# Carried key transposes from unit 6 on, in a gated linear attention and gated MLP kernel with a hand-written early order

## The chip, the cores and the metric

The kernel runs on one core of a Trainium2 chip. The metric is the device time of one execution in microseconds. Five engines each work through a queue of their own: TensorE (PE, its weight loads shown apart as PEld), VectorE (DVE), ScalarE (ACT), GpSimd (POOL) and SyncE (SP), which here only issues DMAs.

## What is computed

```python
def _attn_ref(q, k, v, alpha):            # q, k, v, alpha: [4, 8, 768, 48]
    for t in range(S):
        state = alpha[:, :, t, :, None] * state + np.einsum('bhd,bhe->bhde', k[:, :, t], v[:, :, t])
        y[:, :, t] = np.einsum('bhd,bhde->bhe', q[:, :, t], state)

def _moe_ref(x, w_gate, w_val, w_out):    # x: [3072, 384], d_ff 1536
    gate = 1.0 / (1.0 + np.exp(-(x @ w_gate)))
    return (gate * (x @ w_val)) @ w_out
```

The attention's output, heads side by side, is the MLP's x.

## The kernel before

The 3072 tokens are cut into 6 groups of 512, the 8 heads into 4 pairs. A group and a pair make a **unit**, 24 in all: units 0 to 3 are group 0, units 4 to 7 group 1, units 8 to 11 group 2. In a unit the recurrence is done in chunks: two scans along the tokens on VectorE give the decays G (L422) and F (L426), keys are multiplied by G (L430) and queries by F (L523 in units 0 to 3, L616 later), TensorE makes the scores in a chunk (L535, L632) and the sums of keys and values (L540, L638), VectorE masks the scores (L548, L648), the sums are carried from chunk to chunk (a scan, L450, up to unit 9; eight steps, L670, from unit 10), ScalarE puts the scaled states in place (L563, L659), and TensorE makes the outputs (L575 and L580, or L693).

The MLP is 72 **steps**: 6 groups by 12 tiles of d_ff. A step makes the gate's and the value's product (gv, L245, 18 matmuls of 512 columns), a sigmoid, a product, a split into a high part hh and a low part hl, and 9 matmuls back into po (L738). x has a high and a low part too; for group 0 VectorE makes the low one at L589, one for each of units 1 to 3. Steps 0 and 1 are cut in three by these parts of x.

The weights come as 64-bit numbers, a tile of d_ff in two pieces (tile 0 in three). Each piece is loaded (L374), its top bits are cast (L379 on ScalarE, or L377 on VectorE for pieces listed in CASTS), a word is put together (L382), the high part cast (L385) and the low part subtracted (L393). All of this is done in the first 114 us, along with units 0 to 9, while steps 0 to 11 already run. Raw pieces go round in a ring of four buffers (later three), so a load waits until an older piece's low part is done.

**Keys with tokens on the partitions.** The sums need the decayed keys transposed. Units 0 to 9 do it by `turn` (L460): four 128x128 transposes on TensorE (L464) into a PSUM bank and a copy by ScalarE (L468). Units 10 to 23 do it by `carry` (L472): VectorE transposes 32x32 blocks (L474), one DMA writes them to a way tile in DRAM (L477), and four DMAs bring them back in the right places (L481), in runs of 32 floats.

**Order.** Every piece of work is a numbered part of a plan with an engine, a planned cost, a due time and what it reads and writes. For each engine the table ORDER lists the parts that it runs first, by number, for about the first 140 us; the rest is ordered by planned costs and due times. KEYS and QUERIES name the units whose key or query product runs on VectorE and not on GpSimd. WARM is the number of matmuls on nothing that fill TensorE's queue in the first 30 us.

Numbers in ORDER that matter here (up to 426 the same in both kernels): 119 low x of unit 2, 90 of unit 1, 148 of unit 3 (L589); 329 to 334 the thirds of step 0 and 345 to 350 those of step 1; 316 scores and sums of unit 4; 307 transposes of unit 4. Behind 426 the changed kernel counts four more for each of units 6 to 9.

```python
        if u < 2 * NP:
            t = dict.fromkeys(("load", "more", "G", "dec", "kt", "q", "kn", "X", "A", "mask", "S", "sd", "out", "y"))
            return late(u, g, p, {**t, "flag": 14.0 + u})
...
        if u >= CARRIED:
            t.update(first=x - 0.6, turn=x - 0.4, away=x - 0.2, back=x + 0.6)
...
        carried = "turn" in t
        if carried:
            knn, kn = carry(t, inn, kT, gn, G)
        else:
            pkn, pk = r_gv.next()
            knn, kn = turn(t, inn, kT, pkn, pk)
```

Of the kernel before, what the change touches and what calls it, by code (L numbers as in the profile page):

```python
# [19 lines left out]
B, H, S, D = 4, 8, 768, 48  # L20
# [177 lines left out]
def scan(n):  # L198
    return n / 450
# [6 lines left out]
def act(n):  # L206
    return 0.01 + n / 1065
# [41 lines left out]
def chunked(ctx, tc, rows, vc, vh, vg, weights_in, out, const, ident, flags, weights, within):  # L249
# [185 lines left out]
    def through(u, g, p, t, nch, decn, ends, banks):  # L435
# [6 lines left out]
        plan.add("scalar", 0.09 + act(D * m), t["dec"], lambda: nc.scalar.copy(  # L442
# [4 lines left out]
        for i, (bn, bank) in enumerate(banks):  # L447
            plan.add("scalar", 0.09 + act(D * nch // len(banks)), t["S"], lambda i=i, bank=bank: nc.scalar.copy(
                out=chunks(add, 1 - first + i, m, len(banks)), in_=bank), [bn], [(dn, i)])
        plan.add("vector", 0.09 + scan(D * m), t["S"], lambda: nc.vector.tensor_tensor_scan(  # L450
            out=sd, data0=add, data1=rep, initial=0.0, op0=ALU.add, op1=ALU.mult), [rn, (dn, "i"), *((dn, i) for i in range(2))], [sn], port=True)
        plan.add("gpsimd", 0.25, t["S"], lambda: nc.gpsimd.tensor_tensor(
# [104 lines left out]
    def in_place(u, p, t, qT, inn, vw, A, states):  # L557
# [3 lines left out]
        for j in range(2):  # L561
            r = slice(R * j, R * j + R)
            plan.add("scalar", 0.09 + act((CH - 1) * D), t["sd"], lambda j=j, r=r: nc.scalar.copy(  # L563
                out=sd[r, 1:CH, D * j:D * j + D].rearrange("p c e -> p e c"), in_=some(1, CH)[r].rearrange("p c e -> p e c")), [sn], [(sdn, 2 * j), (sdn, 2 * j + 1)])
# [28 lines left out]
    def late(u, g, p, t):  # L593
# [61 lines left out]
        if u < SCANNED:  # L655
            sn, some = through(u, g, p, t, EH, decn, dec, [
                (pn, bank[:, T // 2:T // 2 + CH * D].rearrange("p (c e) -> p c e", e=D)) for pn, bank in pas])
            for j in range(2):
                plan.add("scalar", 0.09 + act(EH * D), t["sd"], lambda j=j: nc.scalar.copy(  # L659
                    out=vs[own[j], j].rearrange("p c e -> p e c"), in_=some(0, EH)[own[j]].rearrange("p c e -> p e c")), [sn], [(vsn, 2 + j)])  # L660
# [117 lines left out]
    def begin(u):  # L778
# [5 lines left out]
        if u < 2 * NP:  # L784
            t = dict.fromkeys(("load", "more", "G", "dec", "kt", "q", "kn", "X", "A", "mask", "S", "sd", "out", "y"))
            return late(u, g, p, {**t, "flag": 14.0 + u})
# [54 lines left out]
    with tc.manual_schedule():  # L841
# [4 lines left out]
CASTS = ((7, 1), (9, 0))  # L846
QUERIES = (0, 4)
WHOLE = ()
KEYS = (0, 1, 2, 3, 8, 10)
# [10 lines left out]
    ),  # L860
    "vector": (
# [8 lines left out]
    ),  # L870
    "scalar": (
# [6 lines left out]
    ),  # L878
    "gpsimd": (
        5, 2, 3, 72, 0, 56, 101, 4, 1, 130, 305, 312, 374, 141, 367, 322, 326, 83, 388, 112, 432, 392, 425, 486, 493, 449, 453, 554, 510, 514, 623, 779, 611,  # L880
        618, 627, 703, 764, 781,
    ),
    "sync": (
# [7 lines left out]
CARRIED = 10  # L891
# [166 lines left out]
```

## Time and profile before

| | |
|---|---|
| median of 3 runs | 508.27 us (507.75 to 508.96) |
| profiled execution | 508.6 us |
| its span | 506.9 us |
| TensorE busy | 497.2 us (98%) |
| VectorE busy | 322.6 us (64%) |
| ScalarE busy | 193.4 us (38%) |
| GpSimd busy | 85.5 us (17%) |
| TensorE's granted clock, mean over the span | 0.997 |

The profile is of one execution. Its span runs from the first to the last instruction that it shows; 1.7 us lie around it. Shares over the whole span mix two stages: up to about 114 us the weights are unpacked and units 0 to 9 are worked, and behind that only the MLP's steps and the later units are left. A row of a timeline gives start, duration, engine, line, what is written and read, and how many instructions are merged in it. Ends of matmuls are modelled and overlap the next one, so how long TensorE is taken by something is read from start to start.

### The profile page before, as it was taken

The numbers are of one execution on the slowest core, as the hardware profiler recorded it, in microseconds if no ns is written. First come the engines' busy times: TensorE is split into PE (matmuls) and PEld (weight loads), VectorE is DVE, ScalarE is ACT, GpSimd is POOL, SyncE is SP. The second block draws the span as 40 slices with busy tenths as digits, with TensorE's granted clock in tenths as the row PEclk, the third lists the DMA queues.
The fourth block names the chain that finished last, engine by engine and source line by source line (L and its number), as shares of the span: only waits on it lengthen the run. The fifth ranks groups of instructions, "written<-read, shape, count | busy, mean of one in ns | idle before, by whom it ended". The sixth has DMA issues, their size and how long they took to land.

```text
span 506.9 us, 10590 instructions
## 1 busy us (share of the span) xinstructions
PE 497.2 (98%) x4263; PEld 424.7 (84%) x4263; DVE 322.6 (64%) x597; ACT 193.4 (38%) x375; POOL 85.5 (17%) x103
## 2 busy tenths in 40 slices
PE   8999999999999999999999999999999999999995
PEld 3788888888888888888888888888888888888884
DVE  7998989897467956757757658558565432222221
ACT  2888867865323323223233223223322122311221
POOL 3423222211004302203303203112011010000000
PEclk9999999999999999999999999999999999999998
DMA  8797897852553655634535725535733000100001
GB/s 305 264 296 233 274 256 244 249 154 71 127 144 94 152 113 135 154 97 104 132 76 134 196 52 153 123 65 152 166 90 74 12 6 17 63 0 0 1 2 65
DMA packets 81318, 63.92 MB, mean 126 GB/s; under 512 B 62064, under 2 KB 67696, under 8 KB 81264
## 3 DMA queue, kind: packets, MB, share of 16 engines
q1 hardware_dynamic: 81264, 63.20, 45.6%
q8 instruction: 34, 0.56, 0.5%
q14 instruction: 20, 0.16, 0.1%
HBM read 45.62 MB, written 8.39 MB: 107 GB/s over the span
## 4 chain that ended last, share of the span: by engine, by line
PE 88%; ACT 3%; DMA 3%; DVE 3%; issue 1%; SPq 1%; DVEq 0%; ACTq 0%
PE gv L245 51%; PE po L738 26%; PE gv L693 4%; PE at L632 2%; DMA raw<-in_w_dram 2%; PE po L580 1%; PE at L638 1%; DMA x<-yt 1%; ACT vs L659 1%; PE po L575 1%; ACT w L385 1%; DMA in<-in_rows_dram 1%; DVE G L422 0%; PE at L535 0%; DVE sd L450 0%
## 5 line engine op out<-in xcount | busy, mean ns | idle before, releaser
L245 PE MATMUL gv<-x,w 128*128 128x512 f32 x1296 | 300.9, 380 | 0.0
L245 PEld LDWEIGHTS gv<-x,w 128*128 128x128 f32 x1296 | 244.0, 189 | 35.2 <-issue 0.4
L728 DVE TENSOR_TENSOR gv<-gv,sg 128x512 f32<-128x512 f32 x72 | 50.3, 698 | 128.3 <-PE gv L245 121.1
L738 PE MATMUL po<-hh,w 128*128 128x512 f32 x432 | 111.0, 384 | 0.1
L738 PEld LDWEIGHTS po<-hh,w 128*128 128x128 f32 x432 | 79.8, 189 | 12.4 <-ACT hh L729 0.8
L729 ACT CAST hh<-gv 128x512 fp32r<-128x512 f32 x72 | 42.1, 585 | 122.6 <-DVE gv L728 112.2
L726 ACT ACTIVATE sg<-gv 128x512 f32<-128x512 f32 x72 | 43.0, 597 | 113.6 <-PE gv L245 113.5
L677 POOL TENSOR_TENSOR vs<-st,dec 64x384 f32<-64x384 f32 x28 | 29.8, 1063 | 228.6 <-PE gv L245 227.5
L730 DVE TENSOR_TENSOR hl<-gv,hh 128x512 fp32r<-128x512 f32 x72 | 49.1, 681 | 23.1 <-ACT hh L729 19.8
L738 PE MATMUL po<-hl,w 128*128 128x512 f32 x216 | 62.5, 380 | 0.3 <-DVE hl L730 0.3
L738 PEld LDWEIGHTS po<-hl,w 128*128 128x128 f32 x216 | 40.7, 189 | 6.6 <-DVE hl L730 0.9
L648 DVE TENSOR_TENSOR A<-at,mask 64x256 f32<-64x256 f32 x80 | 33.6, 420 | 4.8 <-PE at L638 3.3
L422 DVE TENSOR_TENSOR_SCAN G<-in,d1g 128x512 f32<-128x512 f32 x22 | 31.2, 1418 | 7.6 <-DMA in<-in_rows_dram 7.6
L670 DVE SCALAR_TENSOR_TENSOR st<-st,dec,at 128x48 f32<-128x48 f32 x112 | 29.7, 265 | 3.7
L430 POOL TENSOR_TENSOR in<-in,G 128x512 f32<-128x512 f32 x18 | 24.7, 1370 | 19.7 <-DVE G L422 12.9
L426 DVE TENSOR_TENSOR_SCAN F<-in,d1f 128x512 f32<-128x512 f32 x22 | 27.8, 1264 | 0.2
L693 PE MATMUL gv<-A,vs 112*48 112x64 f32 (+1 forms) x640 | 22.8, 222 | 0.9 <-ACT vs L659 0.8
L693 PEld LDWEIGHTS gv<-A,vs 112*48 112x48 f32 (+1 forms) x640 | 19.4, 123 | 3.9 <-ACT vs L659 2.3
L457 ACT ACTIVATE F<-F 128x512 f32<-128x512 f32 x23 | 14.5, 633 | 4.5 <-DVE in L616 4.4
L632 PEld LDWEIGHTS at<-A,in 48*64 48x64 f32 x640 | 11.2, 134 | 5.9 <-issue 5.6
L616 POOL TENSOR_TENSOR in<-in,F 128x512 f32<-128x512 f32 x6 | 10.0, 1667 | 33.5 <-DVE F L426 33.5
L489 ACT COPY yt<-gv 128x512 f32<-128x512 f32 x20 | 11.7, 587 | 9.5 <-PE gv L693 9.4
(140 smaller groups left out, 339.1 us busy)
## 6 DMA issues: line engine op xcount, KB each, us to landing
in<-in_rows_dram SPq DMA_DIRECT2D x20, 772.5 KB, 5.0
raw<-in_w_dram SPq DMA_DIRECT2D x14, 577.0 KB, 4.9
A<-in SPq DMA_DIRECT2D x40, 128.0 KB, 2.5
first_w<-in_w_dram SPq DMA_DIRECT2D x8, 577.0 KB, 5.0
out_dram<-raw SPq DMA_DIRECT2D x18, 256.0 KB, 2.4
v<-in_vc_dram SPq DMA_DIRECT2D x20, 192.0 KB, 2.7
vs<-in_vh_dram SPq DMA_DIRECT2D x40, 96.0 KB, 3.4
way<-G SPq DMA_DIRECT2D x14, 256.0 KB, 3.2
```

Source lines behind the costliest of these rows:

```text
L245: nc.tensor.matmul(out=dst, lhsT=lhs(a, i), rhs=rhs(b, i), start=(n == 0 and i == 0), stop=(n == len(todo) - 1 and i == NK - 1))
L422: plan.add("vector", scan(n), t["G"], lambda: nc.vector.tensor_tensor_scan(out=G[:, ::-1], data0=az[:, n:0:-1], data1=d1g[size], initial=0 ...
L426: plan.add("vector", scan(n), after(t["G"], 0.01), lambda: nc.vector.tensor_tensor_scan(out=F, data0=az[:, 0:n], data1=d1f, initial=0.0, o ...
L648: plan.add("vector", 0.43, t["mask"], lambda pa=pa, j=j, i=i: nc.vector.tensor_tensor(out=A[other[j], j].rearrange("p (c i t) -> p i c t", ...
L670: nc.vector.scalar_tensor_tensor(out=st[:, c + 1, :], in0=st[:, c, :], scalar=dec[:, c:c + 1], in1=pas[c % 2][1][:, T // 2 + c // 2 * D:T ...
L677: plan.add("gpsimd", pool_(EH * D), t["sd"], lambda j=j: nc.gpsimd.tensor_tensor(out=vs[own[j], j], in0=st[own[j], 0:EH], in1=dec[own[j], ...
L693: nc.tensor.matmul(out=py[R * j:R * j + D, cs], lhsT=vs[r, j, c, :], rhs=A[r, j, cs], start=True, stop=True)
L726: plan.add("scalar", act(T), first(0.3), lambda: nc.scalar.activation(out=sg, in_=got["g"][1][:, 0:T], func=AF.Sigmoid), [got["g"][0]], [sgn])
L728: plan.add("vector", vec(T), first(0.4), lambda: nc.vector.tensor_tensor(out=pv, in0=pv, in1=sg, op=ALU.mult), [sgn], [pvn])
L729: plan.add("scalar", act(T), first(0.45), lambda: nc.scalar.copy(out=hh, in_=pv), [pvn], [hhn])
L730: plan.add("vector", vec(T), first(0.5), lambda: nc.vector.tensor_tensor(out=hl, in0=pv, in1=hh, op=ALU.subtract), [pvn, hhn], [hln])
L738: nc.tensor.matmul(out=pso_now[m][1][:, 0:T], lhsT=weights.part("o", b, f)[:, m * P:(m + 1) * P], rhs=halves(h[a]), start=(f == 0 and i == ...
```

## The change

- CARRIED goes from 10 to 6: units 6 to 9 use `carry` in place of `turn`. Units 6 and 7, which have no due times, get empty ones for its parts.
- KEYS: the key product of unit 4 and of unit 11 goes to VectorE, that of units 3, 8 and 10 to GpSimd. QUERIES: the query product of unit 2 goes to VectorE (the entry 4 has no effect in either kernel, since only units 0 to 3 ask).
- CASTS: the VectorE casts are those of pieces 10.1 and 11.1, not of 7.1 and 9.0.
- Five planned costs are changed; they issue nothing themselves.
- ORDER is new for all five engines. In VectorE's list the third low x (148) stands behind the query product of unit 2 (99 and 101 are unit 2's key and query product), the key product (305) and the 8-column product (304) of unit 4, the reciprocal and the F scan of unit 5 (364, 365) and both word steps of tile 2 (187, 181), which stood behind it or were not VectorE's. In TensorE's list the scores of unit 4 (316) stand ahead of the last thirds of step 0 (331, 334) and step 1 (347, 350). The state scans of units 6 and 7 (L450) stand two weight tiles earlier and one piece-pair earlier in VectorE's list. On SP the return transfers of unit 6 stand behind the loads of pieces 5.0 (215) and 5.1 (221).

```diff
         if u < 2 * NP:
             t = dict.fromkeys(("load", "more", "G", "dec", "kt", "q", "kn", "X", "A", "mask", "S", "sd", "out", "y"))
+            if u >= CARRIED:
+                t.update(dict.fromkeys(("first", "turn", "away", "back")))
             return late(u, g, p, {**t, "flag": 14.0 + u})
...
-CASTS = ((7, 1), (9, 0))
-QUERIES = (0, 4)
+CASTS = ((10, 1), (11, 1))
+QUERIES = (0, 2, 4)
...
-KEYS = (0, 1, 2, 3, 8, 10)
+KEYS = (0, 1, 2, 4, 11)
...
     "tensor": (
...
-        34, 105, 10, 132, 86, 87, 134, 88, 135, 115, 116, 117, 329, 307, 332, 144, 145, 146, 330, 333, 345, 346, 347, 334, 331, 316, 348, 349, 350, 339, 340,
...
+        132, 31, 32, 86, 87, 135, 33, 88, 115, 116, 134, 117, 34, 307, 144, 329, 145, 330, 146, 332, 345, 316, 346, 333, 331, 334, 348, 349, 341, 347, 350,
...
     "vector": (
...
-        153, 107, 154, 157, 111, 300, 166, 137, 90, 301, 140, 159, 302, 160, 303, 169, 136, 119, 171, 362, 172, 363, 175, 148, 187, 177, 304, 364, 178, 365,
...
+        107, 108, 159, 163, 154, 300, 165, 160, 301, 304, 166, 140, 169, 302, 305, 303, 171, 136, 90, 119, 137, 362, 172, 363, 175, 364, 187, 365, 181, 148,
...
     "sync": (
...
+        373, 375, 197, 203, 433, 209, 484, 380, 428, 438, 215, 221, 432, 437, 431, 429, 430, 381, 227, 233, 434, 435, 442, 493, 549, 239, 503, 443, 497, 245,
...
-CARRIED = 10
+CARRIED = 6
```

## Rows read from the trace of the kernel before

**Rows 1.** The page's first line: busy us, share of the span, instructions

```profile
PE 497.2 (98%) x4263; PEld 424.7 (84%) x4263; DVE 322.6 (64%) x597; ACT 193.4 (38%) x375; POOL 85.5 (17%) x103
```

**Rows 2.** Windows by stage: busy us of each engine (instructions), clock, DMA share, GB/s

```profile
3.70:34.10 30.40, 29.00 (x386) 21.40 (x385) 30.17 (x55) 19.34 (x47) 9.61 (x10) 1.00 0.87 310
34.10:66.00 31.90, 31.70 (x378) 26.59 (x377) 29.53 (x48) 27.09 (x50) 10.77 (x12) 1.00 0.81 255
66.00:114.00 48.00, 46.94 (x392) 39.77 (x390) 44.01 (x71) 35.12 (x64) 9.07 (x10) 1.00 0.74 224
114.00:500.00 386.00, 386.00 (x3102) 335.27 (x3102) 217.25 (x414) 109.01 (x211) 53.25 (x57) 1.00 0.37 89
```

**Rows 3.** VectorE's timeline from 33 to 38 us: start, us, line, what

```profile
33.37 0.69 DVE L589 TENSOR_TENSOR x<-po,x 128x512 fp32r<-128x512 f32 x1
34.26 0.95 DVE L382 SCALAR_TENSOR_TENSOR first_w<-first_w,top 128x576 uint32<-128x576 uint32 x1 [0.19 <-ACT top L379]
...
35.17 0.23 DVE L425 RECIPROCAL d1f<-G 128x8 f32<-128x8 f32 x1
...
35.89 1.27 DVE L426 TENSOR_TENSOR_SCAN F<-in,d1f 128x512 f32<-128x512 f32 x1
37.02 0.85 DVE L382 SCALAR_TENSOR_TENSOR raw<-raw,first_w 128x576 uint32<-128x576 uint32 x1
```

**Rows 4.** TensorE's timeline: a run of products, scores of units 4 and 6, transposes

```profile
32.65 4.80 PE L245 MATMUL gv<-x,w 128*128 128x512 f32 x21
37.38 0.69 PE L632 MATMUL at<-A,in 48*64 48x64 f32 x32
...
38.36 2.21 PE L245 MATMUL gv<-x,w 128*128 128x512 f32 x9
...
61.90 0.70 PE L632 MATMUL at<-A,in 48*64 48x64 f32 x32
...
86.70 0.60 PE L464 MATMUL gv<-ident,in 128*128 128x128 f32 x4
87.06 0.46 PE L738 MATMUL po<-hl,w 128*128 128x512 f32 x1
```

**Rows 5.** Moved work by line: ns min/median/max, first and last start, forms

```profile
L474 DVE STREAM_TRANSPOSE G<-in x14: 700/703/705, 127.1 to 373.6; 128x512 f32<-128x512 f32 x14
...
L430 POOL TENSOR_TENSOR in<-in,G x18: 1270/1277/1847, 24.9 to 369.8; 128x512 f32<-128x512 f32 x18
L430 DVE TENSOR_TENSOR in<-in,G x4: 660/672/685, 5.3 to 118.0; 128x512 f32<-128x512 f32 x4
...
L468 ACT COPY kn<-gv x7: 571/586/602, 6.7 to 108.4; 128x512 f32<-128x512 f32 x7
```

**Rows 6.** TensorE's waits, 28 to 115 us: us in total, times, longest

```profile
PE gv L693 <- ACT vs L659: 0.8, 2, 0.6
PE po L738 <- DVE hl L730: 0.3, 1, 0.3
...
PEld gv L693 <- ACT vs L659: 2.3, 5, 0.7
```

**Rows 7.** The chain from 66 to 80 us, and TensorE's wait behind it

```profile
66.75 8.10 DMA raw<-in_w_dram
...
76.82 0.97 DVE sd L450
...
79.62 1.09 PE L693 MATMUL gv<-A,vs 112*48 112x64 f32 x30 [0.57 <-ACT vs L659]
```

**Rows 8.** DMAs: return transfers' issue (ns) and landing (us); KB each and us to landing

```profile
L481 SPq DMA_DIRECT2D kn<-way x56: 318/480/1853, 131.2 to 383.3; - x56
...
DMA to landing us min/median/max: 1.9/4.7/6.6
...
raw<-in_w_dram SPq DMA_DIRECT2D x14, 577.0 KB, 4.9
A<-in SPq DMA_DIRECT2D x40, 128.0 KB, 2.5
```

More of the change, by code (lines that the diff above doesn't have):

```diff
@@ L441, in through @@
         st, stn = sts[p], ("st", p)
-        plan.add("scalar", 0.09 + act(D * m), t["dec"], lambda: nc.scalar.copy(
+        plan.add("scalar", 0.04 + act(D * m), t["dec"], lambda: nc.scalar.copy(
             out=rep.rearrange("p (e c) -> p e c", c=m), in_=ends[:, first:nch + 1].rearrange("p (o c) -> p o c", o=1).broadcast_to([P, D, m])), [decn], [rn])
@@ L447, in through @@
         for i, (bn, bank) in enumerate(banks):
-            plan.add("scalar", 0.09 + act(D * nch // len(banks)), t["S"], lambda i=i, bank=bank: nc.scalar.copy(
+            plan.add("scalar", 0.18 + act(D * nch // len(banks)), t["S"], lambda i=i, bank=bank: nc.scalar.copy(
                 out=chunks(add, 1 - first + i, m, len(banks)), in_=bank), [bn], [(dn, i)])
-        plan.add("vector", 0.09 + scan(D * m), t["S"], lambda: nc.vector.tensor_tensor_scan(
+        plan.add("vector", 0.03 + scan(D * m), t["S"], lambda: nc.vector.tensor_tensor_scan(
             out=sd, data0=add, data1=rep, initial=0.0, op0=ALU.add, op1=ALU.mult), [rn, (dn, "i"), *((dn, i) for i in range(2))], [sn], port=True)
-        plan.add("gpsimd", 0.25, t["S"], lambda: nc.gpsimd.tensor_tensor(
+        plan.add("gpsimd", 0.31, t["S"], lambda: nc.gpsimd.tensor_tensor(
             out=st[:, nch], in0=chunks(add, m - 1, m)[:, 0], in1=chunks(sd, m - 2, m - 1)[:, 0], op=ALU.add), [sn, (dn, "i"), *((dn, i) for i in range(2))], [stn], port=True)
@@ L562, in in_place @@
             r = slice(R * j, R * j + R)
-            plan.add("scalar", 0.09 + act((CH - 1) * D), t["sd"], lambda j=j, r=r: nc.scalar.copy(
+            plan.add("scalar", 0.1 + act((CH - 1) * D), t["sd"], lambda j=j, r=r: nc.scalar.copy(
                 out=sd[r, 1:CH, D * j:D * j + D].rearrange("p c e -> p e c"), in_=some(1, CH)[r].rearrange("p c e -> p e c")), [sn], [(sdn, 2 * j), (sdn, 2 * j + 1)])
@@ L658, in late @@
             for j in range(2):
-                plan.add("scalar", 0.09 + act(EH * D), t["sd"], lambda j=j: nc.scalar.copy(
+                plan.add("scalar", 0.2 + act(EH * D), t["sd"], lambda j=j: nc.scalar.copy(
                     out=vs[own[j], j].rearrange("p c e -> p e c"), in_=some(0, EH)[own[j]].rearrange("p c e -> p e c")), [sn], [(vsn, 2 + j)])
@@ L852 @@
     "tensor": (
[7 rows of a table removed]
[7 rows of a table added]
     ),
     "vector": (
[8 rows of a table removed]
[8 rows of a table added]
     ),
     "scalar": (
[6 rows of a table removed]
[6 rows of a table added]
     ),
     "gpsimd": (
-        5, 2, 3, 72, 0, 56, 101, 4, 1, 130, 305, 312, 374, 141, 367, 322, 326, 83, 388, 112, 432, 392, 425, 486, 493, 449, 453, 554, 510, 514, 623, 779, 611,
-        618, 627, 703, 764, 781,
+        3, 5, 4, 1, 0, 72, 56, 2, 128, 130, 312, 83, 141, 322, 374, 367, 326, 425, 112, 388, 436, 490, 392, 453, 457, 501, 555, 566, 518, 795, 522, 868, 623,
+        634, 639, 643, 940, 703, 719, 797, 798,
     ),
     "sync": (
[4 rows of a table removed]
[5 rows of a table added]
     ),
```

46 rows, old and new, of the table ORDER are left out of this document.

## The prediction

> **What bounds the kernel now.** I read the page's busy line first, then the windows by stage, then the timelines of TensorE and VectorE ahead of 42 us, and last the waits and the chain. TensorE is busy 98% of the span [rows 1]. From 114 us to 500 us it has no idle time at all, 386.00 of 386.00 us; from 34 to 114 us it lacks 1.3 us [rows 2]. So once the products of the weights run, at 32.65 us in an unbroken row [rows 4], the time is the work that stands in TensorE's queue plus the little that it waits, and before that it is the time until that product can start. In the first stage VectorE is the limit: it is busy 30.17 of the 30.40 us from 3.7 to 34.1, and still 93% from there to 66 us and 92% to 114 us [rows 2]. From 114 us on VectorE has 44% to spare, so nothing that the change does to units 10 and 11 is paid for there. The change can gain by taking work off TensorE or by removing its waits ahead of 114 us, and lose by handing VectorE's full first 34 us a worse order.
>
> **Transposes taken off TensorE.** Units 6 to 9 no longer run four transposes each. The set of unit 8 starts at 86.70 and the next matmul at 87.06: 0.36 us of TensorE, although the row says 0.60 (ends are modelled and overlap) [rows 4]. Four sets: −1.4 us, on the path, since no idle time follows them. ScalarE also loses four copies of 0.586 us [rows 5], 2.3 us in a stage where it is 73 to 85% busy [rows 2]; I count that at nothing, because TensorE's waits for ScalarE are counted below.
>
> The Trainium skill ("VectorE: DVE Perf Modes", section "The three transpose paths" and its rules for authors) speaks against the move: TensorE for a 128x128 transpose, at 390 ns, and VectorE for 32x32 blocks alone. By its 390 ns sixteen transposes would be 6.2 us and the sum below −6.1, an estimate; the trace has 0.09 us each, and I go by the trace.
>
> **What takes their place.** VectorE gets four transposes of 0.70 us [rows 5], 2.8 us between about 47 and 100 us. It gives up in the same stage the keys' product of unit 8 (0.67) [rows 5]. Two casts move from pieces 7 and 9 to pieces 10 and 11, still ahead of 114 us, and cancel. Net some 2.1 us of VectorE in the 80 us from 34 to 114, of which it idles 6.4 now [rows 2]. It hides as long as TensorE has other work queued, and costs up to 2.1 if not. The products of units 10 and 11 exchange engines where VectorE has room: nothing; GpSimd's 1.28 us in place of VectorE's 0.67 for unit 10 [rows 5] is covered by the idle GpSimd (9.07 of 48 us busy ahead of 114 us) [rows 2]. SP gets five DMAs for each unit, weighed with the rival below. The planner's changed costs and the empty due times issue no instruction: they order what the lists leave open, all of it behind the stage where TensorE still idles: nothing. Unit 3's keys take 1.28 us on GpSimd in place of 0.67 [rows 5], in a stage where GpSimd is busy a third of the time (9.61 of 30.40) [rows 2] and the fill-in matmuls stand in TensorE's queue behind: nothing, up to 0.6 if TensorE asks at once.
>
> **The head, ahead of 42 us.** The new VectorE order puts seven more instructions ahead of the third low part of x (L589), which the last products of steps 0 and 1 need, and one fewer. Added: the query product of unit 2 and the key product of unit 4 (0.67 each, by the key product's row) [rows 5], an 8-column product and a reciprocal (0.23 each at most), two word pieces of tile 2 (0.95, 0.85) and the F scan of unit 5 (1.27) [rows 3]. Taken away: the key product of unit 3 (0.67, now on GpSimd) [rows 5]. That is 4.87 − 0.67 = 4.2 us; neighbours overlap by 0.1 (35.89 + 1.27 against 37.02) [rows 3], six times 0.1 is 0.6, so 3.6; if the gaps of today's queue go too (0.23 us idle in the stage, and steps apart by less than the overlap), 3.2. Low x then ends at 37.3 to 37.7 in place of 34.06 [rows 3]. TensorE has two covers. Its run of 21 matmuls from 32.65 has twelve at 0.216 before the one that needs that x, until 35.2, which is 1.2 us after 34.06. And the new order puts the scores of unit 4 ahead of it, 1.0 us (37.38 to 38.36) [rows 4]. So the head costs 3.2 − 1.2 − 1.0 = 1.0 us at least and 1.4 by the upper sum; ScalarE stands between VectorE's steps (casts, copies of sums), and two of its instructions late by 0.45 us each would make it 2.3. I take 1.2, near the lower end, because today's queue has nearly no such wait in this stage. The first low x comes some 3.5 us later too, but the transposes of unit 4 and the state products of unit 3 are put ahead of the first product, and what is left of that delay is absorbed by the wait above; it isn't added.
>
> **Waits that may go.** From 28 to 115 us TensorE idles 0.8 us for the scaled states (L659) and 0.3 for the low hidden part; its weight-load side shows 2.3 for the states [rows 6]. The largest of them, at 79.62, goes back to a weight piece: the DMA landed after 8.10 us, its cast and word step followed, the state scan of unit 6 at 76.82 was queued behind them on VectorE, and the copies on ScalarE behind that [rows 7]. The new order runs that scan right behind piece 5.0, two tiles earlier, and unit 7's scan likewise behind the word step of piece 8.0 in place of 9.0; neither stands behind a late weight. I take the visible 0.8 + 0.3 = 1.1 us as gained; the bounds are 2.3 gained (the states' waits of the weight-load side) and nothing, if waits of the same size come elsewhere.
>
> **Sum.** +1.2 − 1.4 − 1.1 = −1.3 us. The profiled execution took 508.6 (span 506.9 and 1.7 around it); it becomes 507.3. The median of the three runs is 508.27, 0.3 lower, so I forecast **507.0**. About 0.2%, 1.0 us, is what a measurement of this kernel can tell from no change; the forecast is just beyond it.
>
> **Rivals.**
> - *The head eats the gain.* VectorE's first queue waits for ScalarE as estimated above, the head costs 2.0, and of the waits only 0.6 goes: +2.0 − 1.4 − 0.6 = 0: 508.3. For it: VectorE has no reserve in that stage [rows 2]. Against it: the later VectorE work is further along when TensorE gets there (the word pieces of tile 2 and a scan are done).
> - *All waits go.* Head 1.0, and the 2.3 us of waits for states vanish: 1.0 − 1.4 − 2.3 = −2.7: 505.6. Against it: VectorE stays over 90% busy, and at that load some step is nearly always late.
> - *The carried keys come late for unit 6* (slower). Its scores wait for the last of four return transfers. On SP these stand behind the loads of pieces 5.0 and 5.1, which wait for the raw buffers that the low parts of tile 3 free. In the new VectorE queue the second of them is eight instructions behind the transpose of unit 6; it is also the 27th behind the third low x, and at 0.615 us each (29.53 us for 48 from 34 to 66 us) that is 16.6 us: 53.9 without waits, 56.3 with the 2.4 us that VectorE idles there [rows 2]. Four issues and a copy among them, 0.48 us each, take 2.4 us, and the landing takes 4.7 in the median, 6.6 at most [rows 8]: there by 61.0 to 65.3. TensorE asks at 61.90 today [rows 4], then at about 61.90 + 1.2 − 0.4 = 62.7. So it holds by 1.7 us at the short end and is 2.6 late at the long one; today's carried units run where the DMA engines are 37% busy, and here it is 81% [rows 2], where the weight load of 4.9 us median took 8.1 [rows 7, 8]. Stretched as much, the median becomes 7.8 and the wait from the early start 53.9 + 2.4 + 7.8 − 62.7 = 1.4; between that and the 2.6 I take 2.0. From the early start it decides once the landing is over 6.4 us, which is why I hold it for less likely than not. +1.2 − 1.4 + 2.0 with no wait gained is +1.8: 510.1.
>
> Beside that: runs of 128 bytes (32 floats) land in 4.7 us, while the copy of twice the size in long rows takes 2.5 [rows 8]. The Trainium skill ("DMA: Bandwidth & Descriptors", section "Specifications") asks for at least 512 bytes for the full rate, and the rows agree in direction; by it the transfers of this change are the costly kind, which is this rival and raises no other price.
>
> **How the numbers follow.** Forecast 0.38, all waits go 0.12, head eats the gain 0.30, late keys 0.20. The forecast's own case reaches, with a head of 1.0 to 1.4 and 0.6 to 1.6 of waits gained, from 506.3 to 507.7; 0.08 of its share is within 0.2%. Of the head's share 0.02 is faster and 0.03 slower. Faster by over 0.2%: 0.30 + 0.12 + 0.02 = 0.44; within: 0.08 + 0.25 = 0.33; slower: 0.20 + 0.03 = 0.23. The range takes in the 505.6 of the fast rival and the 510.1 of the slow one, and below it the 0.5 by which the lowest run of today lies under the median: 505.1 to 510.1.
>
> **What would show it.** Transposes: no L464 rows after unit 5, and 0.36 us less for each. Head: the third L589 ending near 37.5 in place of 34.06, and TensorE idle by a few tenths just ahead of it. Waits: no idle time ahead of L693 for units 6 and 7. Late keys: TensorE's L638 of unit 6 or 7 waiting for a transfer out of the way tile, or L632 of those units idle before it. The forecast is wrong if VectorE idles in the first 34 us by a microsecond or more, if the landing of the return transfers passes 6.6 us, or if the waits for states stay as long as now.

## The result, and the profile after

The changed kernel takes 511.88 us (median of 6 runs, 510.66 to 513.32) where the kernel before takes 508.01 (6 runs): ratio 1.0068, 95% interval 1.0053 to 1.0084, that is 2.7 to 4.3 us slower. The forecast was 507.0, the range 505.1 to 510.1, so the sign was wrong and the time lies outside the range. The profiled execution of the changed kernel took 513.32 us, its span 511.5. It is the longest of the six, 1.4 us above their median, so what its trace shows adds up to more than the 3.5 us of the ratio.

The page's busy line of the kernel after answers to [rows 1], its windows by stage (columns as there) to [rows 2]:

```profile
PE 497.9 (97%) x4247; PEld 423.3 (83%) x4247; DVE 326.3 (64%) x601; ACT 192.7 (38%) x371; POOL 82.8 (16%) x103
```

```profile
3.70:34.10 30.40, 27.87 (x366) 19.38 (x366) 30.09 (x54) 17.94 (x44) 8.13 (x12) 1.00 0.83 299
34.10:66.00 31.90, 30.95 (x381) 25.29 (x379) 31.33 (x52) 26.23 (x50) 10.26 (x10) 1.00 0.88 251
66.00:114.00 48.00, 45.42 (x377) 38.10 (x378) 40.42 (x64) 32.62 (x54) 7.15 (x9) 1.00 0.91 242
114.00:500.00 386.00, 385.86 (x3100) 335.12 (x3099) 221.37 (x421) 112.54 (x219) 54.45 (x58) 1.00 0.39 93
```

The matmuls are 16 fewer, as the change says. Behind 114 us TensorE is as full as before (385.86 of 386.00 us). The loss lies ahead of it: TensorE is busy 1.1 us less in the first window, 0.75 less in the second, 1.5 less in the third. VectorE is now full in the second window too (31.33 of 31.90), and the DMA engines are 0.91 busy in the third, against 0.74.

The waits of TensorE's products from 28 to 115 us in the kernel after (us in total, times, longest) answer to [rows 6]:

```profile
PE po L738 <- ACT hh L729: 1.8, 3, 1.0
PE at L638 <- DMA kn<-way: 1.0, 1, 1.0
PE po L738 <- DVE hl L730: 0.4, 1, 0.4
PE gv L245 <- ACT yt L489: 0.3, 1, 0.3
```

The 0.8 us that TensorE's products waited for states (L693) are gone, as forecast. In their place it waits for the high hidden part (L729, 1.8: 0.55 at 42.44, 0.24 at 98.35, 1.01 at 107.53) and for unit 7's keys out of a transfer (1.0). The 0.3 for the low hidden part is 0.4 now.

To place the loss I use one measure for all kernels, TensorE's lost time: the start of the n-th weights product (L245, 1296 in all), less the work that TensorE had done by then, each matmul at the usual spacing of its line (0.216 us for L245 and L738, 0.0935 for a transpose, and so on; the fill-in matmuls of WARM are not counted as work). The kernel before has lost 12.6 us at the first product, 13.8 at the 46th, 14.4 at the 82nd, 15.9 at the 127th, 16.6 at the 190th and 18.7 at the last. The table gives what each kernel has lost beyond that, in its profiled execution. A kernel that carries four more units has 1.5 us less to do (16 times 0.0935), so its end is later by the last column less 1.5. One execution of each kernel stands behind a row: old_head_3 and old_head_no_transfers have the same head and differ by 0.7 us at the first product, so a difference of that size says nothing by itself.

```
                          1st   46th   82nd  127th  190th   last
after                     2.0    2.9    3.6    4.1    5.3    5.8
new_head                  2.6    3.6    4.9    3.8    3.8    3.8
new_head_early            1.4    3.3    3.2    2.7    2.7    2.9
no_transfers              1.9    2.3    2.7    1.5    1.8    3.0
less_vector               2.0    2.9    2.8    1.6    1.9    2.4
scan_twice                0.0    0.0    1.2    0.8    0.9    1.0
scores_first              1.3    3.0    3.4    2.7    3.5    4.0
no_clash                  1.9    2.8    3.2    2.4    2.6    3.7
old_head_3                0.1    0.4    5.7    5.1    5.4    5.9
old_head_no_transfers     0.8    1.0    6.5    5.3    5.6    6.2
```

The products stand at 28, 49, 63, 82, 104 and 495 us in the kernel before. Of the 5.8 us in the kernel after, 2.0 are lost when the first product starts, 3.6 at the 82nd, and 1.7 more from there to the 190th. Less 1.5 it makes 4.3, and the two spans differ by 4.6.

### The profile page after: what moved, and what is told of

Read it like the earlier page. It is cut to its first block, busy times and chain, and to the rows that moved or that the text cites. A ratio compares the mean times of both kernels' runs of the same rounds, so it can differ in the third digit from the quotient of the medians.

```text
span 511.5 us, 10587 instructions
## 1 busy us (share of the span) xinstructions
PE 497.9 (97%) x4247; PEld 423.3 (83%) x4247; DVE 326.3 (64%) x601; ACT 192.7 (38%) x371; POOL 82.8 (16%) x103
## 4 chain that ended last, share of the span: by engine, by line
PE 77%; DVE 14%; DMA 3%; issue 2%; ACT 2%; DVEq 0%; SPq 0%; ACTq 0%
PE gv L245 46%; PE po L738 25%; PE gv L693 3%; PE at L632 2%; DVE G L422 2%; DVE w L393 2%; DMA raw<-in_w_dram 1%; DMA first_w<-in_w_dram 1%; DVE raw L382 1%; PE at L638 1%; DVE F L426 1%; DVE A L648 1%; DVE sd L450 1%; DVE gv L728 1%; DVE hl L730 1%
## 5 line engine op out<-in xcount | busy, mean ns | idle before, releaser
L245 PE MATMUL gv<-x,w 128*128 128x512 f32 x1296 | 302.1, 380 | 0.5 <-ACT yt L489 0.3
L245 PEld LDWEIGHTS gv<-x,w 128*128 128x128 f32 x1296 | 244.4, 189 | 36.5 <-ACT sg L726 1.0
L738 PE MATMUL po<-hh,w 128*128 128x512 f32 x432 | 111.1, 385 | 1.8 <-ACT hh L729 1.8
L738 PEld LDWEIGHTS po<-hh,w 128*128 128x128 f32 x432 | 79.8, 189 | 14.7 <-ACT hh L729 3.0
L729 ACT CAST hh<-gv 128x512 fp32r<-128x512 f32 x72 | 42.1, 585 | 118.1 <-DVE gv L728 112.2
L677 POOL TENSOR_TENSOR vs<-st,dec 64x384 f32<-64x384 f32 x28 | 31.5, 1126 | 233.6 <-PE gv L245 203.7
L730 DVE TENSOR_TENSOR hl<-gv,hh 128x512 fp32r<-128x512 f32 x72 | 49.0, 681 | 23.6 <-ACT hh L729 18.8
L738 PE MATMUL po<-hl,w 128*128 128x512 f32 x216 | 62.5, 382 | 0.4 <-DVE hl L730 0.4
L738 PEld LDWEIGHTS po<-hl,w 128*128 128x128 f32 x216 | 40.8, 189 | 6.7 <-DVE hl L730 1.0
L422 DVE TENSOR_TENSOR_SCAN G<-in,d1g 128x512 f32<-128x512 f32 x22 | 29.6, 1346 | 6.5 <-DMA in<-in_rows_dram 6.1
L426 DVE TENSOR_TENSOR_SCAN F<-in,d1f 128x512 f32<-128x512 f32 x22 | 26.7, 1214 | 0.1
L430 POOL TENSOR_TENSOR in<-in,G 128x512 f32<-128x512 f32 x18 | 23.0, 1279 | 19.0 <-DVE G L422 8.3
L693 PE MATMUL gv<-A,vs 128*48 128x64 f32 (+1 forms) x640 | 22.0, 222 | 0.0
L693 PEld LDWEIGHTS gv<-A,vs 128*48 128x48 f32 (+1 forms) x640 | 19.0, 123 | 2.5 <-issue 1.2
L632 PEld LDWEIGHTS at<-A,in 48*64 48x64 f32 x640 | 11.1, 134 | 6.3 <-issue 6.2
L489 ACT COPY yt<-gv 128x512 f32<-128x512 f32 x20 | 11.8, 591 | 11.1 <-PE gv L693 9.2
```

The source lines that it names most:

```text
L245: nc.tensor.matmul(out=dst, lhsT=lhs(a, i), rhs=rhs(b, i), start=(n == 0 and i == 0), stop=(n == len(todo) - 1 and i == NK - 1))
L422: plan.add("vector", scan(n), t["G"], lambda: nc.vector.tensor_tensor_scan(out=G[:, ::-1], data0=az[:, n:0:-1], data1=d1g[size], initial=0 ...
L426: plan.add("vector", scan(n), after(t["G"], 0.01), lambda: nc.vector.tensor_tensor_scan(out=F, data0=az[:, 0:n], data1=d1f, initial=0.0, o ...
L677: plan.add("gpsimd", pool_(EH * D), t["sd"], lambda j=j: nc.gpsimd.tensor_tensor(out=vs[own[j], j], in0=st[own[j], 0:EH], in1=dec[own[j], ...
L693: nc.tensor.matmul(out=py[R * j:R * j + D, cs], lhsT=vs[r, j, c, :], rhs=A[r, j, cs], start=True, stop=True)
L729: plan.add("scalar", act(T), first(0.45), lambda: nc.scalar.copy(out=hh, in_=pv), [pvn], [hhn])
```

## The experiments

Two theories stood first. A: the order found anew costs, most of all its first 50 us, and the transfers add a little. B: the transfers cost, the order nothing. Later a third came: VectorE paces the kernel up to 66 us, so that every microsecond which the change gives it there is paid.

**The new head on the kernel before.** Every queue follows the new order up to TensorE's 77th item, about 48 us, then the old one; units 6 to 9 stay on TensorE.

```diff
-KEYS = (0, 1, 2, 3, 8, 10)
+KEYS = (0, 1, 2, 4, 8, 10)
-QUERIES = (0, 4)
+QUERIES = (0, 2, 4)
```

> The first part of the new order on the kernel before: every queue follows the kernel after up to about the first output of unit 4 (TensorE's first 77 items, the same set of items in both kernels; the other engines are cut where they stand at that time), with its engines for keys and queries, and from there the order of the kernel before; units 6 to 9 are turned on TensorE as before, no transfer is added. Theory A (two costs that add: the head about 3 us, the transfers about 1.7 us, less 1.4 us for the transposes): the head's 3 us stay, 508.0 + 3.0 = 511.0. Rival D (the head's idle is lent: later waits of the kernel before take it up, as its own 0.9 us at 48 us and its 2.3 us of waits for states): 508.5 to 509.5.

512.23 us, ratio 1.0081 (1.0067 to 1.0094): 3.4 to 4.8 us slower than the kernel before, without a single transfer added. Theory B falls as the whole cause. The loss is not lent either: 3.6 us at the 46th product are 3.8 at the last, after 4.9 at the 82nd, where the two orders have been joined. TensorE's waits of this kernel from 28 to 115 us:

```profile
PE po L738 <- ACT hh L729: 1.3, 2, 0.7
PE gv L693 <- ACT vs L659: 0.8, 2, 0.6
```

One of the two waits for the high hidden part, 0.59 us at 43.09, is that of the kernel after at 42.44, so it belongs to the new head; the other, 0.73 at 61.38, stands behind the joint. The waits for states are those of the kernel before, so it is the rest of the change that takes them away.

**Half of that head.** The same, cut at TensorE's 50th item, about 30 us.

> The new order up to the end of the start-up alone (TensorE's first 50 items, the same set in both, about 30 us; the first scans of unit 5 on VectorE), then the order of the kernel before. It splits the price of the new head, 4.2 us by the joint at 48 us. If the start-up to the first weights product makes it (2.0 us of TensorE idle more at that point in the kernel after): 510.0 to 510.6. If the stretch from there to 48 us makes it (waits at the first sum over features): 508.0 to 509.

510.66 us, ratio 1.0043 (1.0029 to 1.0058): the start-up alone costs 1.5 to 2.9 us, a little over half of the head. TensorE's timeline there (start, us, engine, line, what, and in brackets the idle time before it and what ended it):

```profile
29.64 0.57 PE L245 MATMUL gv<-x,w 128*128 128x512 f32 x1
31.36 0.70 PE L245 MATMUL gv<-x,w 128*128 128x512 f32 x2 [1.15 <-DVE x L589]
```

The first product starts 1.5 us late and the second waits 1.15 us for the low part of x, which VectorE makes.

**One idle microsecond taken out of the head.** In the kernel after TensorE stands idle at 25 us for the scaled states of unit 2, on ScalarE; the scores of unit 3, 1.09 us from start to start (27.64 to 28.73), are queued behind the products that wait.

```profile
25.98 0.86 PE L575 MATMUL po<-first_w,vs 112*32 112x128 f32 x18 [0.80 <-ACT vs L563]
```

The experiment puts the scores first.

```diff
 "tensor": (
...
-    88, 115, 116, 134, 117,
+    88, 134, 115, 116, 117,
```

> The kernel after with one move in TensorE's queue: the scores of unit 3 (16 products, 1.16 us) go ahead of unit 2's products from states, which in the kernel after stood idle for 1.0 us at 25 us, waiting for ScalarE's copies of the scanned states, while the scores behind them were ready. If an idle microsecond of the head reaches the end (TensorE bounds): first weights product 0.7 to 1.0 us earlier, 510.9 to 511.2. If VectorE sets when the head ends: the first weights product is earlier, but the idle comes back by 48 us, 511.9.

511.74 us, ratio 1.0074 (1.0060 to 1.0089): nothing gained. The first weights product starts 0.7 us earlier, as meant, and the next one waits:

```profile
30.57 0.48 PE L245 MATMUL gv<-x,w 128*128 128x512 f32 x1
31.50 0.70 PE L245 MATMUL gv<-x,w 128*128 128x512 f32 x2 [0.45 <-DVE x L589]
```

By the 46th product the lost time is 3.0 us against 2.9. This idle is not the cause: the low parts of x, which VectorE makes at the same time in both kernels (30.77 and 30.76), end the head when they end it.

**VectorE's clash with GpSimd.** Two of VectorE's instructions ran far beyond their usual time in the kernel after, each beside a product on GpSimd. VectorE's and GpSimd's timelines there:

```profile
21.45 1.55 DVE L450 TENSOR_TENSOR_SCAN first_x<-first_w,first_w 128x192 f32<-128x192 f32 x1 [0.16 <-ACT first_w L448]
...
38.95 1.88 DVE L393 TENSOR_TENSOR w<-raw,w 128x576 fp32r<-128x576 f32 x1
```

```profile
21.31 1.28 POOL L523 TENSOR_TENSOR first_w<-first_w,F 128x512 f32<-128x512 f32 x1 [1.75 <-DVE dec L428]
...
38.95 1.27 POOL L430 TENSOR_TENSOR in<-in,G 128x512 f32<-128x512 f32 x1
```

The scan takes 0.54 us elsewhere, the low word 0.75. The experiment takes both pairs apart.

```diff
 "vector": (
...
-    127, 111, 107, 108,
+    127, 107, 108, 111,
...
-    319, 336, 318, 325,
+    319, 336, 318, 367, 325,
...
 "gpsimd": (
...
-    374, 367, 326,
+    374, 326,
...
-KEYS = (0, 1, 2, 4, 11)
+KEYS = (0, 1, 2, 4, 5, 11)
```

> The kernel after with two moves in the queues: the recurrence scan of unit 2 stands behind two masks instead of ahead of them on VectorE, and the key product of unit 5 is done by VectorE instead of GpSimd. Both take apart pairs that ran at the same time in the kernel after: a VectorE instruction with two inputs in the scratchpad and a GpSimd product, where VectorE's took 1.56 us in place of 0.54 and 1.88 in place of 0.75. Theory A with the clash as its mechanism: the two stretched instructions fall to 0.55 and 0.75 us; 2.15 us of VectorE come back, the added key product costs VectorE 0.67, so up to 1.5 us: 510.4 to 511. Rival (the head is late for VectorE's amount of work and ScalarE's queue, and the clash falls into slack): 511.6 to 512.2.

511.21 us, ratio 1.0070 (1.0052 to 1.0088), the kernel after's own. The scan fell to 0.60 us, but ScalarE's copies behind it still wait for unit 3's sums, at 23.91 as against 23.96. The low word fell to 0.76, but VectorE got a product of 0.70 for it and, at 40.34, stood idle 1.01 us for TensorE. The clash is real and not the cause. With the scores first as well, the ratio was 1.0072 (1.0047 to 1.0097).

**The transfers left out.**

```diff
     def carry(t, inn, kT, gn, G):
-
+        if "cut" in t: return cut(t, inn, kT, gn, G)
...
+    def cut(t, inn, kT, gn, G):
+
+        plan.add("vector", vec(T), t["turn"], lambda: nc.vector.transpose(
...
+        return r_kn.next()
```

> The kernel after, but for units 6 to 9 the transfers away and back are left out (5 DMAs each, 20 in all); VectorE still transposes the blocks, and the state products of these units take whatever keys lie in their buffer, so this part of the output is left undone. It has the whole gain of the change and none of its DMA load. Theory A (the order's first 50 us are the larger part): the wait of unit 7's products (1.0 to 1.4 us) and the late weights near 104 us (1.0 to 1.3 us) go, the DMA share from 66 to 114 us falls from 0.91 to about 0.75: 511.9 - 2.4 = 509.5, still above the kernel before. Rival B (transfers are the whole loss): before less the four sets of transposes, 508.0 - 1.4 = 506.6. Rival C (transfers cost nothing): 511.9.

510.19 us, ratio 1.0041 (1.0029 to 1.0053), against the kernel after's 1.0068: the transfers cost some 1.4 us, and 2.1 us of loss stay without them. The window from 62 to 94 us, first of the kernel after, then without the transfers, then of the kernel before:

```profile
62.00:94.00 32.00, 30.61 (x308) 25.74 (x309) 29.09 (x49) 23.73 (x38) 6.74 (x10) 1.00 0.99 262
```

```profile
62.00:94.00 32.00, 32.00 (x318) 26.77 (x318) 30.61 (x49) 23.96 (x39) 6.17 (x9) 1.00 0.74 234
```

```profile
62.00:94.00 32.00, 31.17 (x290) 26.32 (x290) 29.97 (x49) 23.25 (x42) 7.60 (x9) 1.00 0.83 250
```

With the transfers the DMA engines are 0.99 busy for 32 us and TensorE lacks 1.4 us; without them it lacks nothing.

**The place in SyncE's queue.** Unit 7's returns go ahead of the seventh weight group's loads, the tenth group's loads ahead of unit 8's transfer away.

```diff
 "sync": (
...
-    493, 549, 239, 503, 443, 497, 245, 502, 495, 498, 496, 494,
+    493, 549, 497, 495, 496, 494, 239, 503, 443, 245, 502, 498,
...
-    269, 499, 558, 509, 275, 281,
+    269, 275, 281, 499, 558, 509,
```

> The kernel after with two moves on SyncE's queue alone: the four returns of unit 7 go ahead of the loads of the seventh weight group (from 74.2 to 78 us to some 70 to 73 us), and the two loads of the tenth weight group go ahead of the transfer away of unit 8 and its neighbours. It tells the place in the queue apart from the load on the DMA engines. If the place is the cause: unit 7's state products wait no more for keys (1.0 us) and the weights near 104 us come in time (1.0 to 1.3 us), 510.0 to 510.9, near the kernel without these transfers (510.2). If the load on the engines is the cause (share 0.91 from 66 to 114 us): the waits move to another transfer, 511.5 to 512.5.

518.08 us, ratio 1.0193: much worse, and in two ways. TensorE's waits from 28 to 115 us:

```profile
PE gv L693 <- DMA vs<-in_vh_dram: 4.2, 1, 4.2
PE po L738 <- ACT hh L729: 1.3, 2, 0.7
PE gv L245 <- ACT yt L489: 1.0, 1, 1.0
PE at L632 <- DMA A<-in: 0.7, 1, 0.7
```

Unit 7's keys are no longer waited for; the copy into A that had to stand behind them is, 0.7 us, and a weights product 2 us later waits 1.0 for yt. With the DMA engines 0.95 busy from 62 to 94 us here, another place in the queue handed the wait to another transfer. The 4.2 us come of the second move and tell nothing of the change: the loads of the tenth group wait for a buffer and hold up all that stands behind them on SyncE. It was a poor test of that part.

**The price of VectorE's work ahead of 66 us.** When TensorE comes to the 82nd product, VectorE has done in the kernel after what it had not yet done there before: the query product of unit 2 and the key product of unit 4 (0.61 and 0.55, steps counted without their overlap of 0.08), two transposes (0.62 and 0.63), and unit 7's decay scan with its small steps (1.36), 3.8 us; less the key product of unit 3 (0.58), 3.2. TensorE is 3.0 us later there (65.86 against 62.89). Two runs ask whether that is cause or company. One does a scan of 1.21 us twice in the kernel before:

```diff
-        plan.add("vector", scan(n), after(t["G"], 0.01), lambda: nc.vector.tensor_tensor_scan(
-            out=F, data0=az[:, 0:n], data1=d1f, initial=0.0, op0=ALU.mult, op1=ALU.add), ["d1f", (inn, "a")], [fn], port=True)
+        plan.add("vector", scan(n), after(t["G"], 0.01), lambda: [nc.vector.tensor_tensor_scan(
+            out=F, data0=az[:, 0:n], data1=d1f, initial=0.0, op0=ALU.mult, op1=ALU.add) for _ in range(2 if u == 6 else 1)], ["d1f", (inn, "a")], [fn], port=True)
```

> The kernel before, with one instruction of VectorE done twice: unit 6's scan for the query factors at 51 us, 1.21 us, the same result written again. Nothing else changes. If VectorE paces the stretch up to 66 us, TensorE pays for it: 508.0 + 0.8 to 1.3 = 508.8 to 509.3. If it hides beside TensorE's queue, as the prediction had it for the transposes: 508.0 to 508.2.

509.45 us, ratio 1.0022 (1.0007 to 1.0036), 0.4 to 1.8 us slower. VectorE's and TensorE's timelines:

```profile
50.95 2.48 DVE L426 TENSOR_TENSOR_SCAN F<-in,d1f 128x512 f32<-128x512 f32 x2
```

```profile
58.23 0.70 PE L738 MATMUL po<-hh,w 128*128 128x512 f32 x2 [0.73 <-ACT hh L729]
```

Seven microseconds after the scan TensorE waits for the high hidden part, which ScalarE copies from what VectorE multiplied, and of 1.21 us it has lost 1.2 at the 82nd product and 1.0 at the last. VectorE's work in this stretch is paid for nearly in full.

The other takes the four VectorE transposes out of the kernel without transfers.

```diff
     def carry(t, inn, kT, gn, G):
-
+        if "cut" in t: return r_kn.next()
```

> The kernel after without the transfers of units 6 to 9, as in no_transfers (510.2), and now without their four VectorE transposes either (0.71 us each, two of them ahead of 66 us); the state products of these units take whatever keys lie in their buffer, so this part of the output is left undone. If VectorE paces the stretch: 510.2 - 0.8 to 1.4 = 508.8 to 509.4. If its work hides: 510.2.

509.51 us, ratio 1.0027 (1.0017 to 1.0038) against 1.0041 (1.0029 to 1.0053): about 0.7 us for two transposes of 0.7 ahead of 66 us and two behind it. The intervals overlap; the direction fits the first run, the size is not settled.

**The old head with carried units.** Three kernels join the old head to the new tail. In the first two TensorE waits at the joint, 2.4 us for a late mask (513.08 us) and 3.4 us for late low words of the weights (514.44 us). The third mends both.

> The kernel before up to about 48 us, then the kernel after with units 6 to 9 carried, as in the second graft, but with the low words of the fourth weight group on VectorE ahead of unit 6's decay scan and unit 5's masks, for which TensorE had waited 3.4 us at 52.6 us. If the two costs add: the head's 2.7 us (TensorE idle less at 49 us) stay won, 511.9 - 2.7 = 509.2. If unit 6's keys can't come in time behind the faster head: TensorE waits for them near 62 us by 1 to 4 us, 510.2 to 513.

513.13 us, ratio 1.0095 (1.0076 to 1.0115). Up to the 46th product it has lost 0.4 us, at the 82nd 5.7. TensorE's timeline:

```profile
59.49 1.22 PE L738 MATMUL po<-hh,w 128*128 128x512 f32 x2 [2.71 <-ACT hh L729]
```

The same without the transfers:

> The same order with the transfers of units 6 to 9 left out (the state products of these units take whatever keys lie in their buffer; this part of the output is left undone). If the two costs are the whole loss: the kernel before less the four sets of transposes, 508.0 - 1.4 = 506.6, up to 507.5 with what the joint leaves. If the new tail costs by itself, without transfers and without the new head: 508.5 to 510.

513.30 us, ratio 1.0107 (1.0081 to 1.0133), with the same wait of 2.7 us. So the loss at this joint is not that of the transfers. The timelines of VectorE and ScalarE in old_head_3 show where it starts:

```profile
52.51 0.71 DVE L474 STREAM_TRANSPOSE G<-in 128x512 f32<-128x512 f32 x1 [2.41 <-issue]
```

```profile
52.19 0.22 ACT L432 COPY starts<-G 128x8 f32<-128x8 f32 x1
```

Unit 6's transpose writes over the decays G, from which ScalarE first has to copy, and ScalarE comes to that copy late. So VectorE stands idle for 2.4 us, without the transfers as well, and the steps of the weights' products, which stand behind the transpose in this order, are late by as much. Behind the wait TensorE then ran at half the granted clock for 3.4 us (last section), about 1.6 us more by estimate, half of the 3.11 that it was busy in them. Most of what TensorE gained by 48 us is lost to this joint. Whether the two costs, head and transfers, can be saved one by one stays open: each joint that I made has a cost of its own.

**The old order with carried units, and the new order without.** All four units carried in the old order by hand, with only what the transfers demand moved:

> The change without the new order: the kernel before, with units 6 to 9 carried by hand. Their TensorE transposes and ScalarE copies go; each unit's VectorE transpose stands behind its decayed keys, its five DMAs stand in SyncE's queue where the old order has room, and only what a transfer of some 12 us demands is moved: unit 6's key product on GpSimd, its scan and two masks of unit 5 on VectorE, the decays of units 7, 8 and 9 that read the buffer the transposes write. Theory F (the order found anew is the cost, the carrying is not): 508.0 - 1.4 + the 0.5 to 1 us that unit 6's 0.7 us on a full VectorE may cost = 506.6 to 507.8. Rival G (carrying four units costs by itself, through the load on the DMA engines and VectorE's work in the full stretch up to 66 us, whatever the order): 508.5 to 511.

525.76 us; units 7 to 9 alone 520.21, units 8 and 9 alone 518.21. TensorE's waits of the first from 28 to 115 us:

```profile
PE at L638 <- DMA kn<-way: 3.2, 1, 3.2
PE at L632 <- DMA A<-in: 1.8, 1, 1.8
PE po L738 <- ACT hh L729: 1.6, 2, 1.3
```

Unit 6's keys come 3.2 us late, though its decays were moved up, and the copies behind other returns are late too. This speaks against the theory that the new order is all cost: the carried units need their decays far ahead and room in SyncE's queue, which is what the new order gives them. It doesn't refute it: how much of these 10 to 17 us is my placing isn't told apart, and the first of the three also ran at half the granted clock for 13.6 us (last section).

> The new order of every queue, but units 6 to 9 are again turned by four TensorE transposes each and copied out by ScalarE; no transfer for them, units 10 and 11 are carried as before. It tells the price of the new order apart from the price of carrying. Theory A (the order costs, above all its first 50 us, and the transfers of unit 7 add a wait): the four sets of transposes come back at 4 x 0.36 = +1.4 us, the wait of unit 7's state products for their transferred keys (1.0 to 1.4 us near 84 us) and the late weights near 104 us (1.0 to 1.3 us) go, so 511.9 + 1.4 - 2.4 = about 510.9, still 2.5 us or more above the kernel before. Rival B (the transfers cost, the order nothing): back to the kernel before, 508.0. Rival C (the order alone costs, the transfers nothing): 511.9 + 1.4 = 513.3.

522.63 us, inconclusive: where I put the transposes TensorE stood still, 4.6 us of it in weights products that waited for the hidden part's reader (L730). Each set takes a bank in the rotation that those products use, which is the likely reason; it was not tested. One more kernel, old head and returns ahead in one, took 520.77 us and adds nothing to its two halves. No version beat the kernel before.

## Why the prediction was wrong

**What bounds the kernel** was read rightly, but not used: the text says that VectorE is the limit of the first stage and 93% busy up to 66 us [rows 2], and then gives its added work there a price of nothing.

**Transposes off TensorE, −1.4.** The matmuls are 16 fewer and no L464 follows unit 5. No run isolates the time; by spacing it is 1.5.

**What takes their place, "it hides as long as TensorE has other work queued".** This step failed. Its bound, 2.1 us, was taken over 34 to 114 us with 6.4 us of idle VectorE, but two of the transposes lie ahead of 66 us, where VectorE had 2.4 us to spare and has 0.6 after. scan_twice shows work there paid at 1.0 of 1.21 us.

**The head, +1.2.** This is the term that was furthest off: 2.9 us of lost time at the 46th product, and 3.4 to 4.8 us by the graft. VectorE's low parts of x, the first in the kernel before, then the first two and the third in the kernel after:

```profile
25.78 0.68 DVE L589 TENSOR_TENSOR x<-po,x 128x512 fp32r<-128x512 f32 x1
```

```profile
30.76 1.27 DVE L589 TENSOR_TENSOR x<-po,x 128x512 fp32r<-128x512 f32 x2
...
37.79 0.68 DVE L589 TENSOR_TENSOR x<-po,x 128x512 fp32r<-128x512 f32 x1
```

The first is 5.0 us later, not the 3.5 of the text. The third ends at 38.47, beyond the 37.3 to 37.7 forecast; in no_clash, without the stretched scan ahead of it, it ends at 37.77. But TensorE does not idle just ahead of it. Its losses come earlier and later: 2.0 us before the first product, which the text dropped ("absorbed by the wait above; it isn't added"), and 0.55 at 42.44 for the high hidden part. The text followed one chain, the third low x, with covers on TensorE; when all of VectorE's queue is later, each of its results has to be followed, the first low x and the products' hidden part too. No run takes the moved work out of VectorE's head by itself, so that it is this work which makes the head late is read from the waits. The clash, 2.1 us of VectorE, was not foreseen; taking it out gave nothing.

**Waits, −1.1.** Right for the wait named: no product waits for states, and in new_head, without the new tail, the 0.8 us are back. But waits of the same size came elsewhere, which the text had as a bound: 1.0 for unit 7's keys and 1.0 for a weight load of 7.63 us near 96 us, in place of landings of 4.9 [rows 8] (the kernel before has one load of 8.10 too, [rows 7], but none as late):

```profile
96.51 7.63 DMA raw<-in_w_dram
...
106.28 0.67 ACT w L385
106.95 0.53 ACT hh L729
...
107.53 0.70 PE po L738 x2
```

Without the transfers neither of these two waits is there. With them they don't come in every kernel: no product waits for keys in the traces of scores_first and no_clash, and in scores_first_no_clash one waits 1.6 us.

**The rival of the late keys** had the mechanism. For unit 6 it came true but for the wait itself. The last three returns of unit 6, unit 7's transpose on VectorE, then the state products of both, in the kernel after:

```profile
58.92 1.79 SPq L481 DMA_DIRECT2D kn<-way  x3
```

```profile
64.90 0.71 DVE L474 STREAM_TRANSPOSE G<-in 128x512 f32<-128x512 f32 x1
```

```profile
65.24 0.69 PE L638 MATMUL at<-v,kn 64*48 64x48 f32 x32
...
84.18 0.67 PE L638 MATMUL at<-v,kn 64*48 64x48 f32 x32 [1.02 <-DMA kn<-way]
```

Unit 6's returns land 4.9 to 5.3 us after their issue, the last, issued at 60.22, at 65.1: 2.4 us behind the 62.7 at which the text had TensorE ask. TensorE, itself late, asked at 65.24. That this cost nothing is luck: the loss ahead of it hid the wait. Unit 7's returns took 3.5 to 6.6 us and cost 1.0; the 7.4 beyond its 6.6 was a return of unit 8 and cost nothing. Its time, 510.1, had the small head in it; with the measured one it would have been near 512. As a whole, none of the forecast's cases let the head cost more than 2.3 us.

**The balance.** By ratios: head +4.1 (new_head, its joint included), transfers +1.4, transposes on VectorE +0.7; by rows: off TensorE −1.4, states −0.8. That is +4.0, measured +3.5. It is within the intervals, but sums of grafts need not add, since a joint can cost by itself.

## What to carry to other kernels

When an engine is full in a stretch, price each instruction handed to it there in full (scan_twice: 1.0 of 1.21 us), and count the work that must now be done earlier as well as the work that is new: with two transfers and their places in SyncE's queue, unit 7's keys were there 19 us after their transpose had begun (64.90 to 84.18), so what feeds the transpose is due that much sooner. Idle time of the next engine is then only where the loss shows, and filling one such gap moved it to the next (scores_first). Before reordering a queue of transfers, look at the DMA engines' share in that window: in returns_first, where it was 0.95, a transfer moved ahead made another one late.

## What was not expected of the hardware

VectorE and GpSimd stand in each other's way: the scan that began 0.14 us after GpSimd's product ended 0.41 us after it (23.00 against 22.59), and the low word that began with one ended 0.61 after (40.83 against 40.22), as if each had been held until the product was through. The Trainium skill ("SBUF — State Buffer", section "Who interferes with whom") says that a VectorE instruction with two inputs in SBUF contends with a GpSimd instruction that reads SBUF, and that the port pair which the two share is an exclusive lock; the trace agrees in both places. It works the other way round as well: behind a low word that VectorE began at 83.66, GpSimd's product from 83.88 took 1.65 us, where one without such company took 1.29 (71.61).

A long wait costs TensorE more than itself. In returns_first it stood idle for some 4 us and ran at half the granted clock, the 1.2 GHz level, for the 6 us that followed (windows; the clock is the third figure from the end):

```profile
98.50:103.00 4.50, 0.36 (x2) 0.00 (x0) 3.49 (x6) 2.44 (x4) 1.11 (x1) 0.91 0.91 231
103.00:109.00 6.00, 5.99 (x42) 5.04 (x43) 1.82 (x3) 2.64 (x5) 0.00 (x0) 0.50 0.58 122
```

Shorter waits did it too: that of 2.71 us in old_head_3, and one of 1.63 in scores_first_no_clash. Both, in this order:

```profile
59.20:62.60 3.40, 3.11 (x7) 2.52 (x8) 3.34 (x6) 3.05 (x7) 1.18 (x1) 0.51 1.05 354
```

```profile
82.00:85.00 3.00, 1.17 (x64) 0.91 (x58) 2.57 (x4) 1.18 (x2) 1.16 (x1) 1.00 1.03 269
85.00:88.40 3.40, 3.27 (x8) 2.63 (x9) 2.95 (x6) 2.23 (x5) 0.80 (x3) 0.50 0.78 232
```

That is a part of what the grafts and the hand-made orders lost beyond their waits: old_order_carry_6 has three such stretches, 13.6 us in all at 0.50 (67.5 to 70.9, 105.1 to 108.5 and 122.1 to 128.9). TensorE was busy for 12.3 of them, so by estimate half of that, some 6 us, of its 17 are the clock's. In the kernel after no wait from 28 us on was longer than 1.02 us, and its clock stayed at 1.00 in all four windows.
